# Attention scores by half blocks of queries in array quarters, one double bank per step

## The chip, the cores and the metric

The kernel runs on one core of a Trainium2 chip. The metric is device time in microseconds, the median over runs. Engines are named as in the profile: PE (matmul), PEld (its weight loads), DVE (vector), ACT (scalar), POOL (GpSimd), SP (the queue that issues most transfers).

## What is computed

Windowed attention with four sink keys, then a mixture of experts over its output, all in float32:

```python
B, H, S, D = 4, 8, 768, 64          # n_sink = 4, window = 128
scores = q @ k^T / sqrt(D)
keep = (key < n_sink) | ((0 <= query - key) & (query - key < window))
a = softmax(where(keep, scores, -1e9))
x = (a @ v) as (B * S, H * D) = (3072, 512)
logits = x @ w_gate + log1p(exp(x @ w_noise)) * noise   # 8 experts, top 2, softmax of the two
out = sum over the two experts: weight * (relu(x @ w1[e]) @ w2[e])    # 512 -> 1024 -> 512
```

## The kernel before, in words

Attention runs over 16 pairs of heads (g), each in three steps (jj): 48 steps (n). A step handles 256 queries (two blocks of 128, a = 0 and 1) of the two heads of its pair (h), which makes four units of 128 queries. A query block needs the keys of its own block and of the one before, and the four sinks.

In a step, `qk` (L389) makes the scores of one block a for both heads: the 64 rows of head h of the array hold 128 queries as weights, and 264 columns stream through (132 of the block before with the sinks, 132 of its own). The first block of a head pair has only its own 132. Each block's scores lie in one double bank of PSUM (`S`, one bank per head). `prev` (L392, ACT) copies the 132 old columns to the buffer `cbuf`; `cur` (L399, DVE) puts the own keys over the old ones where the mask `le` allows it (L397 for the first block of a pair). The 128 key slots of a unit are so used twice: an old key leaves the window exactly where an own key enters. `nosink` (L402) and `cur1` (L406), both on POOL, mend the sinks for the first blocks. Then follow `mins` (L409, DVE: row maxima, `mn`), `minus_max` (L412, POOL: `nb`), `exps_sums` (L423, ACT: four exponentials with their sums), `ptr` (L465, PE: eight transposes into bank `P`; L468 for the sinks' probabilities, copied by `pcopy`, L458, POOL), `ptr_c` (L474, ACT: `CT`), `ptr_m` (L484, POOL: `CM`, CT masked to the own keys), `pv` (L494 with v of the old block and L497 with `dv`, the difference of v between neighbouring blocks, made by `dv`, L300), `sinks` (L509), `pv_c` (L517, ACT: output to `xtn`) and `rows` (L523, DVE). After the last pair of a batch come the gate projection (L708), the routing and the writing of rows to memory; between the last steps the first expert rows are gathered. Then the expert stage begins (L1157 to L1229), in which PE multiplies to the end.

The order in attention is written out by hand: `Plan.op` records every operation with its engine, and `Plan.replay` issues them in the order of the table `ORDER`. Each engine works its instructions off in that order. Three double banks (`D`) serve scores, transposes and gate projections in turn, and `replay` picks the bank that is free first. `kind` tells which form of the array a PE operation uses; it enters only the durations with which the order is made. Loads of kq and v go through SP in the order of the table; a buffer of v (two of them) is loaded anew when the step that read it last is done.

## Time and profile before

| | |
|---|---|
| median of 3 runs | 753.51 us (750.51 to 756.1) |
| profiled execution | 756.2 us |
| its span, mean granted clock | 754.6 us, 0.988 |
| busy of the span: PE, PEld, DVE, ACT, POOL | 729.2, 618.4, 418.1, 339.5, 393.6 us |

The span runs from the first instruction to the last; the device time of the same execution is 1.6 us longer. A busy share is an average over two very different stages (attention to about 178 us, experts from there), so it is read by stretch. Matmuls overlap in the records, hence a busy PE may still have room. In the chain of waits a piece is named by its engine, tile and line, with the time it spends on the chain, which for instructions that overlap is their pace.

### The profile page before, as it was taken

Reading aid. Unit: us, or ns where it says so; the run is one execution under the profiler, and the core shown is the slowest. Engines: PE = TensorE matmul, PEld = TensorE weight load, DVE = VectorE, ACT = ScalarE, POOL = GpSimd, SP = SyncE. Lnnn points to the kernel's source line nnn. Section 1 sums busy time; section 2 is a strip of 40 time slices with the busy share of each in tenths; the row PEclk is TensorE's granted clock in tenths of the full one; section 3 lists DMA queues with packets and bytes.
Section 4 is the critical chain, followed back from the end, with each engine's and each line's share of the span. In section 5 each row is a group of like instructions: output and inputs, shape, how many; then the busy total and the mean of one; then the engine's idle time right before and its main releaser. Section 6 shows DMA issues by size and latency. Waiting matters only on the chain.

```text
span 754.6 us, 13413 instructions
## 1 busy us (share of the span) xinstructions
PE 729.2 (97%) x4787; PEld 618.4 (82%) x4787; DVE 418.1 (55%) x1082; ACT 339.5 (45%) x907; POOL 393.6 (52%) x640
## 2 busy tenths in 40 slices
PE   8999899889999999999999999999999999999995
PEld 4766666567889898889889988998899999999994
DVE  5779688786754654654365446535652664473420
ACT  5999799785224413341333243323432441343221
POOL 4346458771237385456636573747284755647212
PEclk9999899989999999999999999999999999999998
DMA  6557687945546743553445354526351653454033
GB/s 227 194 174 221 147 260 170 266 89 153 155 145 145 241 100 60 152 144 63 87 141 132 51 98 144 123 50 154 128 101 28 157 165 62 83 172 74 15 43 43
DMA packets 58310, 97.30 MB, mean 129 GB/s; under 512 B 19296, under 2 KB 31840, under 8 KB 58240
## 3 DMA queue, kind: packets, MB, share of 16 engines
q1 hardware_dynamic: 44864, 68.82, 30.3%
q0 software_dynamic: 13376, 27.60, 20.5%
q8 instruction: 38, 0.62, 0.4%
q14 instruction: 32, 0.26, 0.1%
HBM read 67.99 MB, written 28.40 MB: 128 GB/s over the span
## 4 chain that ended last, share of the span: by engine, by line
PE 77%; ACT 8%; issue 4%; DMA 4%; DVE 3%; POOL 2%; POOLq 0%; ACTq 0%; SPq 0%; DVEq 0%
PE H L1159 11%; PE H L1157 11%; PE H L1158 11%; PE Y L1224 11%; PE Y L1225 11%; PE Y L1223 11%; ACT cbuf L423 4%; PE D L389 3%; PE X L494 1%; ACT cbuf L392 1%; ACT CT L474 1%; PE Y L1228 1%; PE Y L1229 1%; POOL out L1247 1%; PE X L350 1%
## 5 line engine op out<-in xcount | busy, mean ns | idle before, releaser
L1008 POOL DMA_INDIRECT xg<-x_rows,rt_idq x174 | 174.2, 1001 | 60.9 <-issue 51.3
L1204 ACT ACTIVATE h<-H 128x384 fp32r<-128x384 f32 (+4 forms) x127 | 63.8, 503 | 254.5 <-PE H L1159 254.3
L1158 PE MATMUL H<-sqn,w 128*128 128x384 f32 (+4 forms) x508 | 174.0, 343 | 0.9 <-DVE sqn L300 0.9
L1157 PE MATMUL H<-skn,w 128*128 128x384 f32 (+4 forms) x508 | 174.5, 344 | 0.0
L1159 PE MATMUL H<-skn,w 128*128 128x384 f32 (+4 forms) x508 | 174.3, 343 | 0.0
L1212 DVE SCALAR_TENSOR_TENSOR h<-H,h 128x384 fp32r<-128x384 f32 (+4 forms) x167 | 75.1, 470 | 163.7 <-ACT h L1204 163.2
L1247 POOL DMA_INDIRECT out<-y,idx x53 | 93.7, 1767 | 50.5 <-ACT y L1232 34.9
L1256 POOL COPY spacer<-h 1x1 f32<-1x1 f32 x88 | 28.0, 319 | 147.4 <-ACT h L1204 147.2
L1158 PEld LDWEIGHTS H<-sqn,w 128*128 128x128 f32 x508 | 95.4, 188 | 7.7 <-DVE sqn L300 1.2
L1157 PEld LDWEIGHTS H<-skn,w 128*128 128x128 f32 x508 | 95.4, 188 | 7.4 <-ACT skn L1075 0.4
L1159 PEld LDWEIGHTS H<-skn,w 128*128 128x128 f32 x508 | 95.3, 188 | 2.1
L423 ACT ACTIVATE cbuf<-cbuf,nb 128x132 f32<-128x132 f32 x192 | 75.6, 412 | 2.4 <-POOL nb L412 2.4
L1225 PE MATMUL Y<-w2a,h 128*128 128x512 f32 x192 | 75.6, 394 | 0.0
L1225 PE MATMUL Y<-w2b,h 128*128 128x512 f32 x192 | 75.6, 394 | 0.0
L1224 PE MATMUL Y<-w2a,h 128*128 128x512 f32 x192 | 75.5, 393 | 0.0
L1224 PE MATMUL Y<-w2b,h 128*128 128x512 f32 x192 | 75.5, 393 | 0.0
L1223 PE MATMUL Y<-w2b,h 128*128 128x512 f32 x192 | 75.1, 391 | 0.0
L1223 PE MATMUL Y<-w2a,h 128*128 128x512 f32 x192 | 74.8, 389 | 0.0
L389 PE MATMUL D<-kq 64*128 64x264 f32 (+1 forms) x384 | 57.1, 406 | 9.2 <-DVE cbuf L399 3.6
L1075 ACT ACTIVATE skn<-xtn 128x512 fp32r<-128x512 f32 (+2 forms) x46 | 27.8, 605 | 58.5 <-DVE xtn L1066 58.4
L389 PEld LDWEIGHTS D<-kq 64*128 64x128 f32 x384 | 31.6, 192 | 21.1 <-DVE cbuf L399 6.0
L399 DVE COPY_PREDICATED cbuf<-le,D 128x256 f32<-128x256 uint8 x80 | 34.7, 445 | 18.4 <-ACT cbuf L392 17.8
(210 smaller groups left out, 1203.8 us busy)
## 6 DMA issues: line engine op xcount, KB each, us to landing
st<-in_w1l SPq DMA_DIRECT2D x32, 512.0 KB, 4.4
st<-in_w2l SPq DMA_DIRECT2D x32, 512.0 KB, 4.1
kq<-in_kq SPq DMA_DIRECT2D x15, 792.0 KB, 6.5
out<-zt SPq DMA_DIRECT2D x31, 256.0 KB, 5.6
vn<-in_v SPq DMA_DIRECT2D x16, 384.0 KB, 5.8
x_rows<-xr SPq DMA_DIRECT2D x48, 128.0 KB, 5.0
xg<-x_rows,rt_idq POOLq DMA_INDIRECT x174, 2.8
out<-y,idx POOLq DMA_INDIRECT x53, 5.1
```

Of the source, the lines that this page charges most:

```text
L389: nc.tensor.matmul(p[:, :2 if j else 1], kq(g)[r, j // 2, 2 + j % 2, NS:], x[:, :2 if j else 1], start=True, stop=True)
L423: nc.scalar.activation(C(n)[:, u], C(n)[:, u], AF.Exp, bias=get("nb", n)[:, u:u + 1], scale=1.0 / math.sqrt(D), accum_out=get("sm", n // 2 ...
L1008: nc.gpsimd.indirect_dma_start(out=x[:, i, :], out_offset=None, in_=xbuf.rearrange("r (q d) -> (r q) d", d=sh.SW), in_offset=bass.Indirect ...
L1157: nc.tensor.matmul(p, w[:, 0], xh, start=(i == 0), stop=False)
L1158: nc.tensor.matmul(p, w[:, 0], xl, start=False, stop=False)
L1159: nc.tensor.matmul(p, w[:, 1], xh, start=False, stop=(i == sh.DM // 128 - 1))
L1204: nc.scalar.activation(get("h", FC * q + f, [128, 2 * 128 * FIRST], F32R)[:, :width], H(q, f), AF.Relu)
L1212: nc.vector.scalar_tensor_tensor(h[:, o:o + s1 - s0], p[:, s0:s1], 0.0, h[:, s0:s1].bitcast(F32), op0=OP.max, op1=OP.subtract)
L1223: nc.tensor.matmul(p, hh, w[:, 0], start=(f == 0), stop=False)
L1224: nc.tensor.matmul(p, hh, w[:, 1], start=False, stop=False)
L1225: nc.tensor.matmul(p, hl, w[:, 0], start=False, stop=(f == FC - 1))
L1247: d = nc.gpsimd.indirect_dma_start(out=out, out_offset=bass.IndirectOffsetOnAxis(ap=c["idx"][:size(e, t), e, t:t + 1], axis=0), in_=get("y ...
```

## The change

The 128 queries of a block are split in halves (i). A score matmul now uses a quarter of the array: 64 rows of head h by 64 columns of queries, and 196 key columns. For the first half these are the old block, the sinks and the own block's first 64 keys in one piece; for the second half the last 64 old keys with the sinks (68 columns) and then all 128 own keys, whose first 64 are written straight over slots that the window has left. Scores of a whole step lie in one double bank, one bank per head. `prev` becomes one copy of four units (132 columns each), `cur` two predicated copies, each of 64 partitions, all units and 64 columns. The first block of a pair gets one addition of a mask (`cur0`), and `nosink` goes. kq is laid out anew in memory for this, with as many bytes.

The order is new throughout. `SIDE` says for some operations which of two engines they go to, and `BANKS` which bank each use takes. `dv` is on POOL for all pairs (before, for every second two), `ptr_m` on DVE for four of every twelve steps. By `SIDE`, 5 of 48 score copies, 2 CT copies and 5 output copies move from ACT to DVE, 9 `pcopy` from POOL to ACT, and 12 `minus_max`, 6 additions to the sums and one `cur1` from POOL to DVE. In front of the diff's core the tables themselves are left out.

```diff
-PR = dict(load_qk=0.0, load_v=24.264, w1=36, pc_pool=0, gap_8=1, dv_pool=2, et=42, cm_pool=12, gap=4, subs=0)
+PR = dict(load_qk=0.0, load_v=24.264, w1=36, pc_pool=0, gap_8=1, dv_pool=4, et=42, cm_pool=8, gap=4, subs=0)
...
 ORDER = """
...
+"""
+SIDE = """
...
+"""
+BANKS = """
...
 """
...
+        if alt:
+            self.alts.append((i, (eng, dur, kind), alt))
+            if SIDE.replace("\n", "")[len(self.alts) - 1:len(self.alts)] == "1":
+                eng, dur, kind = alt
+            fn.__defaults__ = fn.__defaults__[:-1] + (eng,)
...
-                    x = self.slot[kx] = len(r) - 1 if kx in last else min(range(len(r)), key=lambda x: r[x])
+                    x = self.slot[kx] = int(banks[len(self.slot)]) if banks else len(r) - 1 if kx in last else min(
+                        range(len(r)), key=lambda x: r[x])
...
-                d = (d + (0 if k % 3 == kind % 3 else .2 if k == 1 else .15)) * (2 if t < self.cold else 1)
+                d = (d + (0 if k % 4 == kind % 4 else .2 if k == 1 else .15)) * (2 if t < self.cold else 1)
...
-    def qk(n, a):
-        g, j, _ = at(n, 2 * a)
-        for h in range(2):
-            r = slice(h * D, (h + 1) * D)
-            p = get("S", 2 * n + a, [128, 2, 512], F32, "ps")[:, h, :2 * KW].rearrange("p (a b) -> p a b", a=2)
-            x = keys(g, max(j - 1, 0))[r]
-            nc.tensor.matmul(p[:, :2 if j else 1], kq(g)[r, j // 2, 2 + j % 2, NS:], x[:, :2 if j else 1], start=True, stop=True)
-
-    def prev(n, a):
-        nc.scalar.activation(C(n)[:, 2 * a:2 * a + 2, :], get("S", 2 * n + a)[:, :, :KW], AF.Copy)
-
-    def cur(n, a):
-        c, p = C(n)[:, 2 * a:2 * a + 2, NS:], get("S", 2 * n + a)
-        if at(n, 2 * a)[1] == 0:
-            nc.vector.tensor_tensor(c, p[:, :, NS:KW], m0[:, None, :].to_broadcast([128, 2, 128]), op=OP.add)
+    def scores(n):
+        return get("S", n, [128, 2, 512], F32, "ps")[:, :, :2 * BW].rearrange("p h (a k) -> p a h k", a=2)
+
+    def qk(n):
+        for a in range(2):
+            g, j, _ = at(n, 2 * a)
+            for i in range(2):
+                for h in range(2):
+                    r, t = slice(h * D, (h + 1) * D), slice(64 * i, 64 * i + 64)
+                    k, x = kq(g)[r, 0].rearrange("p b k -> p (b k)"), scores(n)[t, a, h]
+                    w, k0 = kq(g)[r, 1, j, t], KW * (j - 1)
+                    if not j or not i:
+                        o = x if j else x[:, :KW]
+                        nc.tensor.matmul(o, w, k[:, k0:k0 + BW] if j else k[:, :KW], start=True, stop=True)
+                    else:
+                        nc.tensor.matmul(x[:, 64:KW], w, k[:, k0 + 64:k0 + KW], start=True, stop=True)
+                        y = x[:, :64]
+                        y = bass.AP(tensor=y.tensor, offset=y.offset, ap=[list(y.ap[0]), [KW, 2], [1, 64]])
+                        nc.tensor.matmul(y, w, k[:, k0 + KW:k0 + KW + 128].rearrange("p (a k) -> p a k", a=2), start=True, stop=True)
+
+    def moved(eng, out, x):
+        if eng == "DVE":
+            nc.vector.tensor_copy(out, x)
         else:
-            nc.vector.copy_predicated(c, le[:, None, :].to_broadcast([128, 2, 128]), p[:, :, KW + NS:2 * KW])
-
-    def nosink(n):
-        nc.gpsimd.memset(C(n)[:, :2, :NS], -BIG)
-
-    def cur1(n):
-        c = C(n)[:, 2:, NS:2 * NS]
-        nc.gpsimd.tensor_tensor(c, c, m1[:, None, :].to_broadcast([128, 2, NS]), op=OP.add)
+            nc.scalar.activation(out, x, AF.Copy)
+
+    def small(eng):
+        return nc.gpsimd if eng == "Pool" else nc.vector
+
+    def old(n):
+        return int(n % NJ == 0)
+
+    def units(n):
+        return C(n).rearrange("p (a h) k -> p a h k", a=2)
+
+    def prev(n, eng):
+        moved(eng, units(n)[:, old(n):], scores(n)[:, old(n):, :, :KW])
+
+    def cur0(n):
+        nc.vector.tensor_tensor(units(n)[:, 0], scores(n)[:, 0, :, :KW], m0[:, None, :].to_broadcast([128, 2, KW]), op=OP.add)
+
+    def cur(n, i):
+        r = slice(64 * i, 64 * i + 64)
+        c = units(n)[r, old(n):, :, r]
+        nc.vector.copy_predicated(c, le[r, None, None, :].to_broadcast([64, 2 - old(n), 2, 64]), scores(n)[r, old(n):, :, KW:])
+
+    def cur1(n, eng):
+        c = C(n)[:, 2:, :NS]
+        small(eng).tensor_tensor(c, c, m1[:, None, :].to_broadcast([128, 2, NS]), op=OP.add)
...
+            need = {jj, max(jj - 1, 0)}
+            op("PE", .68 if jj else .61, n + P(g, "qk"), lambda n=n: qk(n), r=[("kq", g, i) for i in need], w=[("S", n)],
+               u=[("kq", g), ("C", n)], kind=3)
+            op("ACT", .46 if jj else .27, n + P(g, "prev"), lambda n=n, e=0: prev(n, e), r=[("S", n)], w=[("C", n, 0)], u=[("C", n)],
+               alt=("DVE", .61 if jj else .34, 0))
             if not jj:
-                op("Pool", .05, n + P(g, "nosink"), lambda n=n: nosink(n), w=[("C", n, 0)], u=[("C", n)])
-            for a in range(2):
-                z = n + .2 * a
-                s = 2 * n + a
-                need = [jj] if not jj or a else [jj - 1, jj]
-                op("PE", .45 if jj or a else .26, z + P(g, "qk"), lambda n=n, a=a: qk(n, a),
-                   r=[("kq", g, i) for i in {jj, *need}], w=[("S", s)], u=[("kq", g), ("C", n)], kind=1)
-                if jj or a:
-                    op("ACT", .27, z + P(g, "prev"), lambda n=n, a=a: prev(n, a), r=[("S", s)], w=[("C", n, a)], u=[("C", n)])
-                op("DVE", .335, z + P(g, "cur"), lambda n=n, a=a: cur(n, a), r=[("S", s)], w=[("C", n, a)], u=[("C", n)])
+                op("DVE", .34, n + P(g, "cur"), lambda n=n: cur0(n), r=[("S", n)], w=[("C", n, 0)], u=[("C", n)])
+            for i in range(2):
+                op("DVE", .335 if jj else .2, n + P(g, "cur"), lambda n=n, i=i: cur(n, i), r=[("S", n)], w=[("C", n, 0)], u=[("C", n)])
             if not jj:
-                op("Pool", .15, n + .4 + P(g, "cur1"), lambda n=n: cur1(n), w=[("C", n, 1)], u=[("C", n)])
-            op("DVE", .62, n + .4 + P(g, "mins"), lambda n=n: mins(n), r=[("C", n, 0), ("C", n, 1)], w=[("mn", n)], u=[("C", n)])
+                op("Pool", .15, n + .4 + P(g, "cur1"), lambda n=n, e=0: cur1(n, e), w=[("C", n, 0)], u=[("C", n)], alt=("DVE", .085, 1))
...
+               alt=None if odd else ("DVE", .6, 0))
...
+    kq = np.zeros((B * HP, 128, 2, NB, 128 + NS), np.float32)
+    for i, x in enumerate((k, q)):
+        kq[:, :, i, :, :128] = x.reshape(B, HP, 2, NB, 128, D).transpose(0, 1, 2, 5, 3, 4).reshape(B * HP, 128, NB, 128)
+    kq[:, :, 0, :, 128:] = kq[:, :, 0, :1, :NS]
```

How the rows stand on the engines. SP at the start of the program (vr are the sinks' values), before:

```order
L356 DMA vr<-in_vs 16x1024 x2
L367 DMA vn<-in_v 128x768
L364 DMA kq<-in_kq 128x528 x3
L364 DMA kq<-in_kq 128x1584 x2
L367 DMA vn<-in_v 128x768
L690 DMA nz<-in_noise 128x192
```

and now:

```order
L379 DMA kq<-in_kq 128x2x264 x3
L379 DMA kq<-in_kq 128x1584
L382 DMA vn<-in_v 128x768
L379 DMA kq<-in_kq 128x1584
L371 DMA vr<-in_vs 16x1024 x2
L382 DMA vn<-in_v 128x768
L728 DMA nz<-in_noise 128x192
```

The loads of kq, which stood behind vr and the first v, are the queue's first.

PE in attention, some four steps after the first gate projection, before (L389 scores, L465 and L468 transposes, L494 and L497 the products with v, L509 sinks):

```order
L465 MATMUL D<-idf,cbuf 128x64 x8
L389 MATMUL D<-kq 128x264 x4
L465 MATMUL D<-idf,cbuf 128x64 x8
L468 MATMUL D<-idf,pcbuf 128x64 x2
L389 MATMUL D<-kq 128x264 x4
L465 MATMUL D<-idf,cbuf 128x64 x8
L494 MATMUL X<-CT,vn 64x128 x4
L497 MATMUL X<-CM,dv 64x128 x4
```

and now, at about the same step (L406 to L411 scores, L500 and L503 transposes, L529 and L532 products with v, L544 sinks):

```order
L544 MATMUL X<-ps,vr 128x128 x4
L500 MATMUL D<-idf,cbuf 128x64 x16
L503 MATMUL D<-idf,pcbuf 128x64 x2
L406 MATMUL D<-kq 64x196 x2
L408 MATMUL D<-kq 64x68
L411 MATMUL D<-kq 64x2x64
L408 MATMUL D<-kq 64x68
L411 MATMUL D<-kq 64x2x64
L406 MATMUL D<-kq 64x196 x2
L408 MATMUL D<-kq 64x68
L411 MATMUL D<-kq 64x2x64
L408 MATMUL D<-kq 64x68
```

What was four matmuls per step among the transposes is now a run of twelve, in pieces of 196, 68 and 2x64 columns, in an array form of its own.

ACT at about the same steps, before (L392 score copies, L423 exponentials, L474 CT, L501 sinks' probabilities, L517 output):

```order
L474 ACTIVATE CT<-D 128x512
L392 ACTIVATE cbuf<-D 128x2x132
L423 ACTIVATE cbuf,sm<-cbuf,nb 128x132 x4
L501 ACTIVATE ps<-D 128x128
L474 ACTIVATE CT<-D 128x512
L392 ACTIVATE cbuf<-D 128x2x132 x2
L517 ACTIVATE xtn<-X 128x256 x2
L423 ACTIVATE cbuf,sm<-cbuf,nb 128x132 x4
L392 ACTIVATE cbuf<-D 128x2x132
```

and now (L417 stands for every plain copy, L458 exponentials, L536 sinks' probabilities):

```order
L417 ACTIVATE cbuf<-D 128x4x132
L458 ACTIVATE cbuf,sm<-cbuf,nb 128x132 x4
L417 ACTIVATE xtn<-X 128x256 x2
L417 ACTIVATE CT<-D 128x512
L417 ACTIVATE cbuf<-D 128x4x132
L417 ACTIVATE cbuf<-D 128x2x132
L458 ACTIVATE cbuf,sm<-cbuf,nb 128x132 x4
L417 ACTIVATE CT<-D 128x512
L536 ACTIVATE ps<-D 128x128
```

Two copies of 2x132 elements have become one of 4x132; the rest of a step's work on ACT stands there as before.

## Rows read from the trace of the kernel before

**Rows 1.** Busy time of each engine by stretch (us, count), granted clock, DMA share

```profile
core 0: us, PE busy (x) PEld busy (x) DVE busy (x) ACT busy (x) POOL busy (x), PEclk, DMA share, GB/s
...
20.00:40.00 20.00, 19.77 (x256) 14.68 (x254) 14.54 (x37) 19.95 (x86) 7.34 (x27) 1.00 0.55 186
...
60.00:80.00 20.00, 18.76 (x259) 14.05 (x259) 18.61 (x69) 19.64 (x85) 12.82 (x37) 1.00 0.75 175
...
140.00:160.00 20.00, 15.83 (x172) 11.05 (x172) 16.21 (x67) 17.25 (x67) 15.40 (x40) 0.91 0.44 120
...
sum 180.00, PE 163.41 PEld 115.03 DVE 132.45 ACT 152.34 POOL 99.49; mean PE 18.16 PEld 12.78 DVE 14.72 ACT 16.93 POOL 11.05
...
176.00:746.00 570.00, 568.80 (x2859) 505.47 (x2858) 288.75 (x687) 188.09 (x298) 293.15 (x378) 1.00 0.46 110
```

**Rows 2.** Chain of waits, 14 to 76 us (start us, us, what)

```profile
19.43 0.48 ACT CT L474
...
21.91 0.55 ACT cbuf L392 x2
22.45 1.50 ACT cbuf L423 x8
...
25.03 0.27 ACT xtn L517
```

**Rows 3.** Chain of waits, 46 to 60 us

```profile
47.96 1.16 PE D L389 x8
...
49.36 0.59 PE X L494 x8
49.95 0.44 PE X L497 x8
...
52.99 0.87 PE D L389 x8
53.86 0.24 PE D L465 x8
```

**Rows 4.** PE in order of time, 50.31 to 50.34 us

```profile
50.31 0.42 PE L708 MATMUL D<-xtn,wbd 128*32 128x256 f32 x4
```

**Rows 5.** Groups, 0 to 180 us (count, busy us, mean ns, idle before)

```profile
L789 ACT ACTIVATE rt_ex<-rt_ab 128x48 f32<-128x48 f32 x3 | 0.7, 244 | 0.4 <-DVE rt_ab L787 0.3
...
L399 DVE COPY_PREDICATED cbuf<-le,D 128x256 f32<-128x256 uint8 x80 | 34.7, 445 | 18.4 <-ACT cbuf L392 17.8
...
L397 DVE TENSOR_TENSOR cbuf<-D,m 128x256 f32<-128x256 f32 x16 | 6.7, 419 | 4.7 <-PE D L389 3.8 <-ACT cbuf L423 0.5
L300 DVE TENSOR_TENSOR dv<-vn 128x640 f32<-128x640 f32 x8 | 6.5, 812 | 2.8 <-DMA vn<-in_v 2.8
...
L300 DVE TENSOR_TENSOR sqn<-D,skn 128x512 fp32r<-128x512 f32 x4 | 2.7, 676 | 0.3 <-ACT skn L1075 0.3
...
L450 DVE RECIPROCAL ri<-sm 128x4 f32<-128x4 f32 x16 | 1.8, 153 | 0.5 <-POOL sm L436 0.5
...
L484 POOL TENSOR_SCALAR_AFFINE_SELECT CM<-CT 128x512 f32<-128x512 f32 x32 | 21.3, 666 | 9.5 <-ACT CT L474 3.7 <-issue 3.0 <-POOL CM L484 0.8
L300 POOL TENSOR_TENSOR dv<-vn 128x640 f32<-128x640 f32 x8 | 12.4, 1546 | 4.2 <-DMA vn<-in_v 4.2
```

**Rows 6.** POOL's waits, 14 to 178 us (total, times, longest), and landing of v

```profile
POOL dv L300 <- DMA vn<-in_v: 2.1, 2, 1.3
...
DMA to landing us min/median/max: 3.4/5.8/9.6
```

**Rows 7.** SP in order of time, and the chain of waits, start

```profile
0.93 0.87 SPq L356 DMA_DIRECT2D vr<-in_vs  x2
...
2.30 2.33 SPq L364 DMA_DIRECT2D kq<-in_kq  x5
...
1.25 5.42 PE X L350 x13
```

**Rows 8.** Chain of waits, 70 to 86 us

```profile
75.60 6.11 DMA vn<-in_v
```

## What the change is predicted to do

> **What bounds the kernel now.** I first read the busy time of each engine by stretch [rows 1]. From 176 us to 746 us PE is busy 568.80 of 570 us at granted clock 1.00: that is the expert stage, and the change does not touch it. The change lives in the attention stage, roughly the first 178 us, so it can only move the moment at which the expert matmuls begin; whatever it gains there comes off the end one for one, and nothing else does. Within attention the reader is to see two halves. From 20 to 80 us ACT has no idle time: 19.95 us of the first 20, 19.64 of the last. PE is close behind (19.77 and 18.76, though matmuls overlap in these figures), and DVE goes from 14.54 to 18.61. After that no engine is full all the time: at 140 to 160 us ACT shows 17.25, DVE 16.21, PE 15.83 of 20, with a granted clock of 0.91. Then I read the chain of waits. In the first half it runs along ACT nearly without a break: four exponentials with their sums take 1.50, two score copies 0.55, a copy of turned probabilities 0.48, a copy of the output 0.27 [rows 2]. In the second half it jumps between engines and includes pure transfer waits such as 6.11 us for v at 75.60 [rows 8]. So the first half is a matter of ACT work, the second of PE work, of order and of late transfers. All sums are made against the profiled execution, 756.2 us (span 754.6); the median of the runs shown, 753.51, lies 2.7 below it.
>
> **The change part by part.** *Score matmuls.* A full step now streams 2 blocks of 264 columns, two head halves side by side; eight instructions take 0.87 us when PE is in the right array form already, 1.16 when it enters it after a wait [rows 3]. That is 0.22 us per 264-column pass. With 196 columns a pass is 0.22 x 196/264 = 0.163, and a quarter streams four of them in a step: 0.65. Two of the quarters have each pass in two pieces (68 and 128 columns). Small passes cost little beside their columns: eight transposes of 64 columns, two side by side, take 0.24 [rows 3], so 0.060 a pass where 64 columns stream in 0.053; four more pieces add 4 x 0.007, which makes 0.68. [...] This holds if the four quarters run side by side. For that the trace has a near relative: the gate projection puts four column strips of the array to work, and all four first passes fall in one window of 0.03 us [rows 4]. So a full step saves 0.87 - 0.68 = 0.19, times 32 = 6.1 us; the 16 first steps of a head pair (132 and 264 columns before, 132 and 196 now) save 2 x 0.22 x 68/264 = 0.11 each, 1.8 in all. Together -7.9 us of PE.
>
> *Array forms.* Before, scores, transposes and sinks use one form of the array (64 rows by 128 columns, or 16 of them), so PE goes from one to another without a break: the transposes behind the scores take 0.24 for eight [rows 3]. Now scores have a form of their own. Counted along PE's order, changes of form in attention go from 128 to 149. The price of one is read from two neighbours of the same size: the eight matmuls of CT, entered from the transposes, take 0.59, the eight of CM behind them 0.44 [rows 3], so 0.15. 21 x 0.15 = +3.2 us. Net on PE: -7.9 + 3.2 = -4.7. Bounds: -1.8, if a change is as dear as the 1.16 row makes it (21 x 0.29 = 6.1), and -7.9, if it is entered for nothing. In the first half PE hides behind ACT; half of the steps, -2.3, fall in the second, where PE shares the chain. I take -1.5.
>
> *ACT.* One copy of 528 elements replaces two of 264. Two of them take 0.55 [rows 2], a copy of 512 takes 0.48, so one of 528 about 0.50: -0.05 a step. Of 80 short copies 13 short and 30 long remain: 22.0 becomes 18.6. Two CT copies (0.48) and five output copies (0.27) go to DVE: -2.3. Nine small copies of sink probabilities come from POOL; the nearest ACT row is a 128x48 exponential, 0.244 [rows 5]: +2.2. ACT loses 3.5 us in all. Counted along the table SIDE, 2.9 of these lie in the first 24 steps, where ACT sets the pace: 0.8 from merging, 2.8 from moved copies, less 0.7 for three sink copies. On the path I take -2.5, between -1.0 (the merging alone) and -3.5.
>
> *DVE.* It gets sixteen masks of turned probabilities (12 of 512 elements at 0.676, as the subtraction that reads PSUM, and 4 of 256 at 0.419), +9.8; it loses eight v differences (0.812), -6.5; ten PSUM copies come in, +6.1 by the same two rows; nineteen tiny operations at 0.153, +2.9 [rows 5]. The predicated copies stay at 256 elements per partition, since a half block uses 64 partitions and all four units: 64 of them at 0.445 and 32 of half the size (between 0.25 and 0.445, I take 0.31) for 80 before, +2.8. Together +15 on the 132.45 of the first 180 us [rows 1]. ACT hides this where DVE stands at 14.54 of 20, but not at 60 to 80 us. There four steps' masks (2.4) come in and two v differences (1.6) go out: +0.8. That is what I take; bounds 0, and +5 if a third of it lands on the path.
>
> *POOL.* All sixteen v differences are now its own, +8 x 1.546 = 12.4, against sixteen masks of at most 0.666 and some forty operations of about 0.2 that leave. Its sum falls a little. But each difference waits for a v transfer, whose median is 5.8 us from issue to landing [rows 6], and behind it on POOL stand the negated maxima, for which ACT's exponentials wait. Before, behind the start, POOL waited 2.1 us for v in two places [rows 6] and DVE 2.8 [rows 5], and DVE's waits stop the score buffers: the 6.11 us in [rows 8] ends in such a difference, with predicated copies queued behind it. I take 0: the same lateness moves from one queue to another. Bounds: -4.9 (both sums gone) and +10 (the POOL rival below, less the part that ACT's queue absorbs).
>
> *Start.* kq is now issued ahead of the sink values and v; its issues began at 2.30 us, and the queue's first at 0.93 [rows 7]: up to -1.4. The warming matmuls ahead of the first scores fall from 13 to 5; 13 of them take 5.42 us, to 6.67 [rows 7], with the first scores right behind them, so scores no longer wait for them. But five end at 3.3 us, and the first scores may then run at the lower clock level: up to +2.0 for three steps of 0.68. I take -0.8. The buffers change too (one double bank per step instead of two), which removes waits of scores for a bank; these are short in the first half and I price them at nothing, since ACT is full there.
>
> Sum: -1.5 (PE) -2.5 (ACT) +0.8 (DVE) +0 (POOL) -0.8 (start) = **-4.0 us**. 756.2 becomes 752.2; on the median 753.5 becomes 749.5.
>
> **The rivals.** *More than that.* Part of the second half are waits of an engine's whole queue for a transfer, as the 6.11 us for v [rows 8]. The order is new everywhere, so such a wait could vanish (-5 of it, since v is needed some time anyway), and PE's full -4.7 count instead of -1.5: 753.5 - 4.0 - 5 - 3.2 = 741.3. For it: DVE no longer holds v differences at all. Against it: other waits may appear, and v loads stand no further ahead of their use than before.
>
> *Nothing to be had.* Scores get cheaper, but ACT, not PE, evacuates them at 19.9 of 20; only merging helps, -0.8 to -1.0, and DVE's +0.8 eats it: 753.5. [...] The full ACT in [rows 1] agrees for the first half.
>
> *Slower through POOL.* Fourteen v differences behind the first two each wait for their transfer on POOL, and negated maxima, exponentials, transposes follow late. It decides from 0.8 us per group on: 14 x 0.8 = 11 us outweighs the 4.0 by more than 7.5. At 1.0 us per group: 753.5 - 4 + 14 = 763.5. For it: 2.1 us over two waits is 1.05 each [rows 6]. Against it: only two of the eight differences on POOL waited behind the start.
>
> *Slower through the passes.* If a quarter's two passes go before the next quarter starts, the overlap is mostly lost: eight quarter blocks of 0.163 are 1.3 us instead of 0.68, 0.43 above the 0.87 of before; 48 x 0.43 + 3.2 = 24 us, of which PE's slack hides some: 753.5 + 18 = 771. With part of the overlap lost PE loses from 0.80 us a step on (3.2/48 = 0.07 below 0.87); midway, at 1.0, it is 48 x 0.13 + 3.2 = 9.4, about 762. [...] Four first passes inside 0.03 us [rows 4] speak against it, though there the strips are columns alone, not quarters.
>
> **How the numbers follow.** The three runs before span 750.51 to 756.1, so about 1% (7.5 us) is what can be told from no change. Forecast (-8 to 0): 0.54. More than that: 0.25. Nothing to be had: 0.09. POOL: 0.07. The passes: 0.05. Faster by over 1% (below 746.0) is the second case and the lowest edge of the first: 0.28. Slower (above 761.0) is the two last, nearly whole: 0.11. Within: 0.61. The range reaches down to the second case, 741, and up to where POOL's waits just eat the gain and DVE's +5 is added, 758; it leaves out some 0.1 on either side. The forecast's own range is 745 to 753.
>
> **What would show it.** In the profile after: score matmuls of a full step in some 0.7 us behind one another (1.1 or 1.3 shows the passes' case); long score copies of about 0.50 pace on ACT; ACT still 19 or more of 20 from 20 to 70 us, with the expert matmuls beginning near 174 instead of 178; DVE near 147 us in its first 180; POOL's waits for v near 5 us in all (14 shows the POOL case). Wrong would be the forecast if ACT has room from 20 to 80 us: then something else sets the pace, and my ACT and PE terms change places.

## The result and the profile after

The changed kernel takes 758.5 us (median of 20 runs, 755.07 to 765.51) against 753.5 for the one before (20 runs beside them): a ratio of 1.0069, 95% interval 1.0050 to 1.0087. A second set gave 760.07 against 755.52, ratio 1.0064 (1.0035 to 1.0093). So it is slower by 0.7%, about 5 us, where 4 us less had been forecast. That is inside the 1% called no change, and just above the range (758.0). One yardstick for all that follows: the kernel before, measured against itself on the same chip, gave 0.9966 (0.9943 to 0.9989), an interval that leaves out 1 though both kernels are the same. So ratios that differ by less than some 0.35% (2.6 us) are not told apart here.

The profiled execution is the shortest of the twenty: 755.07 us, span 753.5. It is even 1.1 us shorter than the profiled one of before. Its rows show how the work changed; how much time the change costs they do not show, and this is a first lesson of the case. These are the stretches that answer to [rows 1] (columns: length, busy time and count of each engine, granted clock, DMA share, GB/s):

```profile
core 0: us, PE busy (x) PEld busy (x) DVE busy (x) ACT busy (x) POOL busy (x), PEclk, DMA share, GB/s
...
20.00:40.00 20.00, 19.55 (x356) 15.87 (x351) 18.04 (x46) 17.27 (x71) 7.55 (x16) 1.00 0.52 162
40.00:60.00 20.00, 16.64 (x312) 12.34 (x310) 16.90 (x42) 18.46 (x78) 8.39 (x21) 1.00 0.78 226
60.00:80.00 20.00, 18.38 (x363) 14.75 (x359) 18.55 (x68) 19.34 (x78) 11.22 (x27) 1.00 0.85 199
...
100.00:120.00 20.00, 14.51 (x274) 11.98 (x275) 16.90 (x64) 16.28 (x64) 14.60 (x34) 0.91 0.59 157
...
sum 180.00, PE 154.15 PEld 116.55 DVE 152.34 ACT 148.05 POOL 90.08; mean PE 17.13 PEld 12.95 DVE 16.93 ACT 16.45 POOL 10.01
...
176.00:746.00 570.00, 566.74 (x2831) 504.56 (x2831) 287.01 (x683) 186.90 (x296) 294.51 (x377) 1.00 0.47 110
```

The reader is to see that the work moved the way that the forecast gave: PE from 163.41 to 154.15, ACT from 152.34 to 148.05, DVE from 132.45 to 152.34. But ACT, 19.95 of 20 before, has room at 20 to 60 us, and no engine took its place: PE, DVE and ACT all stand between 16.6 and 19.6. The prediction had named just this as the sign that it was wrong.

The chain of waits, which ran along ACT in [rows 2], now winds through DVE with its masks and predicated copies:

```profile
31.78 0.61 ACT cbuf L417
...
32.43 0.61 ACT CT L417
...
33.06 0.69 DVE CM L516
...
33.78 0.47 DVE cbuf L437
...
34.28 0.70 DVE mn L444
...
35.01 0.44 DVE xtn L415
...
35.47 0.77 DVE xr L558 x2
```

The scores themselves did what they were priced at. Here are two full steps in a row, PE in order of time (start, length, line, operation, count):

```profile
66.78 0.46 PE L500 MATMUL D<-idf,cbuf 64*128 64x64 f32 x8
67.17 0.38 PE L406 MATMUL D<-kq 64*64 64x196 f32 x2
67.19 0.34 PE L408 MATMUL D<-kq 64*64 64x68 f32 x4
...
68.42 0.38 PE L411 MATMUL D<-kq 64*64 64x128 f32 x3
68.73 0.46 PE L500 MATMUL D<-idf,cbuf 64*128 64x64 f32 x8
```

From 67.17 to 68.73 are 1.56 us for two steps. A single step followed at once by other matmuls takes 0.88 to 0.89 from its first start to the next one's, so the second step costs 0.67 to 0.68 (forecast: 0.68) and the change of array form 0.21. Of the 32 full steps 17 stand alone in PE's order; such a step takes no less than the 0.87 of [rows 3]. The matmuls of the two columns of quarters start 0.02 us apart (67.17 and 67.19).

And the groups of the first 180 us that answer to [rows 5] (shapes, count, busy, mean ns, idle before):

```profile
L437 DVE COPY_PREDICATED cbuf<-le,D 64x256 f32<-64x256 uint8 x64 | 28.5, 454 | 2.3 <-ACT cbuf L417 1.2
L437 DVE COPY_PREDICATED cbuf<-le,D 64x128 f32<-64x128 uint8 x32 | 9.6, 301 | 0.4
...
L516 DVE TENSOR_TENSOR CM<-D,ge 128x512 f32<-128x512 f32 x12 | 8.3, 691 | 3.3 <-ACT CT L417 2.0 <-issue 0.7 <-PE D L500 0.4
...
L417 ACT ACTIVATE cbuf<-D 128x528 f32<-128x528 f32 x30 | 18.2, 611 | 7.5 <-PE D L411 7.1
...
L312 POOL TENSOR_TENSOR dv<-vn 128x640 f32<-128x640 f32 x16 | 24.8, 1550 | 4.5 <-DMA vn<-in_v 4.1 <-PE D L503 0.2
```

Each price in them is within 0.02 us of the one used; only the long copy's record lasts 0.61 us, but where work follows at once, the next instruction mostly starts 0.49 to 0.52 us after it (forecast: 0.50). POOL waits 4.1 us for v, some 5 were forecast.

### The profile page after: what moved, and what is told of

Same layout as the page of the kernel before. It is cut to its first block, busy times and chain, and to the rows that moved or that the text cites. A ratio compares the mean times of both kernels' runs of the same rounds, so it can differ in the third digit from the quotient of the medians.

```text
span 753.5 us, 14768 instructions
## 1 busy us (share of the span) xinstructions
PE 717.7 (95%) x5491; PEld 618.5 (82%) x5491; DVE 437.4 (58%) x1139; ACT 334.8 (44%) x872; POOL 386.1 (51%) x588
## 4 chain that ended last, share of the span: by engine, by line
PE 74%; DVE 10%; ACT 7%; issue 5%; DMA 2%; POOL 1%; POOLq 0%; DVEq 0%; ACTq 0%
PE H L1195 11%; PE H L1197 11%; PE H L1196 11%; PE Y L1262 11%; PE Y L1263 11%; PE Y L1261 10%; ACT cbuf L458 3%; DVE cbuf L437 2%; DVE mn L444 2%; DMA st<-in_w1l 2%; PE D L406 1%; DVE xr L558 1%; PE Y L1266 1%; POOL out L1285 1%; PE Y L1267 1%
## 5 line engine op out<-in xcount | busy, mean ns | idle before, releaser
L1046 POOL DMA_INDIRECT xg<-x_rows,rt_idq x174 | 176.0, 1011 | 61.1 <-issue 51.4
L458 ACT ACTIVATE cbuf<-cbuf,nb 128x132 f32<-128x132 f32 x192 | 75.3, 403 | 5.9 <-POOL nb L447 4.0
L406 PE MATMUL D<-kq 64*64 64x196 f32 (+1 forms) x448 | 41.5, 339 | 3.9 <-DVE cbuf L437 1.2
L312 DVE TENSOR_TENSOR w<-st,w 128x1024 fp32r<-128x1024 f32 x30 | 36.7, 1223 | 13.9 <-ACT w L1151 13.4
L1183 DVE TENSOR_TENSOR gw<-xg,perm 32x8 f32<-32x8 f32 x174 | 27.5, 158 | 26.0 <-DMA xg<-x_rows,rt_idq 21.9
```

The lines of the kernel that those rows point to most:

```text
L406: nc.tensor.matmul(o, w, k[:, k0:k0 + BW] if j else k[:, :KW], start=True, stop=True)
L458: nc.scalar.activation(C(n)[:, u], C(n)[:, u], AF.Exp, bias=get("nb", n)[:, u:u + 1], scale=1.0 / math.sqrt(D), accum_out=get("sm", n // 2 ...
L1046: nc.gpsimd.indirect_dma_start(out=x[:, i, :], out_offset=None, in_=xbuf.rearrange("r (q d) -> (r q) d", d=sh.SW), in_offset=bass.Indirect ...
```

## The experiments

All medians are device microseconds beside runs of the kernel before on the same chip. The first two rows repeat the result.

| kernel | median | before | ratio (95%) |
|---|---|---|---|
| changed | 758.5 | 753.5 | 1.0069 (1.0050 to 1.0087) |
| after_again | 760.07 | 755.52 | 1.0064 (1.0035 to 1.0093) |
| before_again | 752.82 | 755.89 | 0.9966 (0.9943 to 0.9989) |
| form_only | 755.61 | 755.89 | 0.9990 (0.9969 to 1.0012) |
| order_only | 764.86 | 755.89 | 1.0112 (1.0086 to 1.0137) |
| keep_busy | 762.86 | 755.89 | 1.0081 (1.0056 to 1.0107) |
| dv_dve | 761.66 | 755.35 | 1.0085 (1.0052 to 1.0119) |
| side0 | 762.33 | 755.35 | 1.0091 (1.0062 to 1.0119) |
| cm_pool | 760.37 | 755.35 | 1.0073 (1.0045 to 1.0102) |
| moves_only | 766.16 | 755.35 | 1.0150 (1.0109 to 1.0191) |
| mid_order | 758.68 | 755.52 | 1.0039 (1.0018 to 1.0061) |
| tail_order | 759.89 | 755.52 | 1.0054 (1.0034 to 1.0074) |
| mid_tail | 757.92 | 755.52 | 1.0032 (1.0006 to 1.0058) |
| act_twice | 764.77 | 752.80 | 1.0160 (1.0142 to 1.0177) |
| dve_twice | 769.08 | 752.80 | 1.0203 (1.0173 to 1.0233) |
| pe_twice | 769.03 | 752.80 | 1.0206 (1.0181 to 1.0232) |
| before_act_twice | 767.98 | 752.80 | 1.0179 (1.0133 to 1.0226) |
| form_nb | 761.73 | 754.00 | 1.0113 (1.0086 to 1.0139) |
| before_nb | 753.45 | 754.00 | 1.0003 (0.9979 to 1.0027) |

**The three parts apart.** The change has a form (quarters, one bank, merged copies), an order, and moves of work between engines. In form_only the changed kernel's operations stand at the places that before's order gives them, on the engines of before:

```diff
-PR = dict(..., dv_pool=4, ..., cm_pool=8, ...)
+PR = dict(..., dv_pool=2, ..., cm_pool=12, ...)
 ORDER: each operation at the place of its counterpart in the order of before
 SIDE:  all 0;  BANKS: whichever is free
```

> The new form of the scores alone (quarters, 196 columns, one bank per step, merged copies), in the order of before and with every operation on the engine that had it before. If the form is what it was priced at: PE -4.7 of which 1.5 on the path, ACT -0.8 by merging, DVE's smaller predicated copies up to +2.8 busy, so 751 to 754 us, ratio 0.996 to 1.001. If the form is what costs (changes of array form, passes in turn, predicated copies on half the partitions): ratio 1.007 or more, like the whole change.

Measured 755.61, ratio 0.9990 (0.9969 to 1.0012): the form alone changes nothing that can be told, though the 2.3 us that the forecast had for it (1.5 for PE, 0.8 for merging) lie just at the edge of the interval. order_only has the new order and form with the engines of before (the same lines of PR and SIDE, ORDER as changed except that eight masks stand behind the copy they then read, BANKS as changed).

> The new form and the new order, with every operation on the engine that had it before (half of the v differences back on VectorE, all masks on GpSimd, the 40 moved operations moved back). If the moves onto VectorE cost (its busy time in the first 180 us went from 132 to 152 us): 2 to 5 us below the changed kernel, ratio 0.999 to 1.004. If the moves paid, as I had forecast for ScalarE (-2.5): 2 to 4 us above the changed kernel, ratio 1.010 to 1.012.

It is 0.45% above the changed kernel, little more than the yardstick: 1.0112 against 1.0069 and 1.0064. So the moves seem to pay some 3.4 us within the new order, and the new order with the old engines costs 9 us over form_only. moves_only is form_only with the moves (dv_pool=4, cm_pool=8, SIDE as changed, masks on DVE right behind their copies).

> The new form and the engines of the change (all v differences on GpSimd, a third of the masks on VectorE, the 40 moved operations), but in the order of before; banks taken as they come free. It is form_only plus the moves. If the new order by itself is what costs, and the moves pay as they did between order_only and the changed kernel (some 4 us): 750 to 753 us, ratio 0.993 to 0.998, faster than both. If moves and order only work together: 756 us or more, ratio 1.002 or more.

With the moves in the old order the kernel loses 10.5 us against form_only (766.16 to 755.61), where 750 to 753 us had been expected of the moves alone. Either alone is dear, 9 and 10.5 us, and together they cost 5. The order was made for the moved work, and neither can be priced by itself. What is shown is that order and moves together cost the 0.7%, and that the form does not. The table of banks belongs to the order and was not tried by itself.

**The moves one by one.** dv_dve changes `dv_pool=4` to 2 alone, cm_pool changes `cm_pool=8` to 12 and puts eight masks behind the copy they then read, side0 puts the 40 ones of SIDE to 0.

> The changed kernel with half of the v differences back on VectorE, as before; nothing else. In the trace of the changed kernel one of them holds GpSimd for 1.51 us at 103.43, and behind it a negated maximum comes late, ScalarE waits 1.7 us for that, TensorE stands for 2.9 us and its clock falls. Theory A (such differences on GpSimd cost where a maximum waits behind them): 1 to 3 us below the changed kernel, ratio 1.003 to 1.006. Theory B (VectorE is the bound, and eight differences of 0.81 are 6.5 us more for it): 2 to 5 us above it, ratio 1.009 to 1.013.

> The changed kernel with the 40 operations of the table of sides back on the engines that had them before (copies on ScalarE, sums, negations and sink copies on GpSimd); the v differences and the masks stay where the change put them. If these moves off ScalarE pay (forecast: 2.8 us of its first 24 steps): 2 to 4 us above the changed kernel, ratio 1.010 to 1.012. If VectorE is the bound of the first half now (18.0 of 20 us at 20 to 40): 1 to 4 us below, ratio 1.002 to 1.005.

> The changed kernel with all masks of turned probabilities on GpSimd, as before; they read the copy that ScalarE makes, not the bank. Takes 10 us from VectorE and gives GpSimd sixteen operations of 0.41 to 0.65. If VectorE is the bound: 1 to 4 us below the changed kernel, ratio 1.002 to 1.005. If GpSimd's queue is what delays (negated maxima behind long operations there): 1 to 5 us above, ratio 1.008 to 1.013.

1.0085, 1.0091, 1.0073: all at or above the changed kernel, none of them clear of it. Taking back no single one of the moves helps. That does not show that they cost nothing where they are, since work taken back burdens another queue: in cm_pool ACT waits 7.9 us for negated maxima from POOL, in the changed kernel 4.0 (first 180 us).

**The clock.** Each run lists the mean granted clock. In the twenty runs of the changed kernel the span grows by 0.72 us for each us of clock lost (span times one minus the clock), correlation 0.91 (0.84 us in the runs of before, correlation 0.80). This is read from the spread of the runs; no run sets the clock by itself. before_again is the kernel before, unchanged; keep_busy adds dummies to the changed one:

```diff
     def ptr(n):
         p = get("P", n, [128, 2, 512], F32, "ps")
+        for i in range(2 if n >= 24 else 0):
+            nc.tensor.matmul(p[:, 1], cst["one"], cst["one"][:, None, :].to_broadcast([128, 4, 128]), start=True, stop=True)
```

> The kernel before, unchanged, to get the granted clock of many of its runs. In twenty runs of the changed kernel the span goes with the clock: from 754.4 us at 0.996 to 763.9 at 0.98, some 0.7 us of span for each us of clock that is lost (1 minus the clock, times the span). Theory A (the change loses work time and also lets the clock fall more often): the runs of before show a median clock near 0.992 to 0.994, and at an equal clock they lie some 2 us below the changed kernel. Theory B (the clock is the same and all 5 us are work): median clock 0.988 as in the changed kernel, and at equal clock 5 us below it.

> The changed kernel with two more dummy matmuls of 512 columns ahead of the transposes of each of the last 24 steps; they write the bank that the transposes then overwrite, so they run in TensorE's waits, and cost at most 24 x 0.43 = 10 us where it does not wait. If falls of the granted clock after TensorE's pauses cost the time (0.72 x 9 us lost in the median run): median clock 0.992 or more, 2 to 6 us below the changed kernel, ratio 0.999 to 1.004. If the clock is not the cause: no gain, ratio 1.007 to 1.02.

The changed kernel lost a mean of 8.9 us of clock in 20 runs and 11.1 in 12 more; before lost 7.6 over the 119 runs of it that list their clock. The difference of 2.1 is worth 0.72 x 2.1 = 1.5 us. With 0.72 times the lost clock taken off each span, the changed kernel stands at 750.9 and 750.6, before at 747.8: some 3.0 us are work (2.7 with 0.84 in place of 0.72). Theory A, then, with both parts. By the same subtraction form_only stands at 749.1, order_only at 754.4 and moves_only at 753.7 (6.8, 11.4 and 14.5 us of clock lost): only about half of what order and moves cost alone is work. The dummies did raise the clock (6.3 us lost), but the time did not fall (0.1 to 0.2% above, which can't be told from no change), as was expected if the clock is not the cause. With the clock taken off, keep_busy stands at 756.6: some 6 of the 10 us of dummy work came through, more than 0.72 x 3.4 = 2.4 us could return. So this run neither shows nor refutes the share of the clock.

**Two places in the new order.** By a count of finished attention work the profiled execution is some 3 us ahead of before at 105 us (maxima, exponentials, copies, masks, differences and routing steps; 1 us without the routing), and by 110 us nothing of this is left. In another order such a count is a rough measure. PE there, and POOL and DVE just before:

```profile
105.59 0.45 PE L866 MATMUL D<-m,one 128*128 128x56 bf16 x12
108.98 0.46 PE L500 MATMUL D<-idf,cbuf 64*128 64x64 f32 x8 [2.95 <-DVE rt_ro L923]
110.26 0.59 PE L406 MATMUL D<-kq 64*64 64x196 f32 x2 [0.82 <-DVE cbuf L437]
```

```profile
102.79 0.64 POOL L519 TENSOR_SCALAR_AFFINE_SELECT CM<-CT 128x512 f32<-128x512 f32 x1 [0.79 <-ACT CT L417]
103.39 1.54 POOL L312 TENSOR_TENSOR dv<-vn 128x640 f32<-128x640 f32 x1
104.91 0.22 POOL L447 TENSOR_SCALAR nb<-mn 128x4 f32<-128x4 f32 x1
```

```profile
102.33 0.69 DVE L444 TENSOR_REDUCE mn<-cbuf 128x4 f32<-128x528 f32 x1
...
103.80 1.20 DVE L851 TENSOR_TENSOR m<-oh 128x48 bf16<-128x48 f32 x1
```

The maxima are done at 103.0, their negation waits until 104.91 behind a mask and a v difference of 1.54, and the exponentials, an output copy, the row transposes and a bank's release on DVE follow late in turn, each first in its own queue. PE stands for 2.95 us. The eight transposes right behind that still take 0.46, as elsewhere; behind one more wait of 0.82 the granted clock is 0.50, and a 196-column score matmul takes 0.54 to 0.59 instead of 0.33 to 0.38 (columns as in the stretches above, the clock is the 0.50):

```profile
111.00:112.00 1.00, 1.00 (x26) 1.00 (x23) 0.91 (x4) 0.15 (x2) 0.90 (x5) 0.50 0.06 16
```

after_again shows whether that belongs to the order:

> The changed kernel, unchanged, for a second profiled execution and for more granted clocks beside runs of before on the same chip. The first profiled execution was the shortest of twenty (755.07 us, clock 0.994) and was 6 us ahead of before at 105 us, then gave it back between 105 and 118 us and after the last exponential. If those two places belong to the order: the same two places lose again (TensorE idle for 2 us or more between 100 and 116 us, 11 us or more from the last exponential to the first expert matmul, 7.2 in the order of before), and the median is 757 to 760 us. If they were chance: other places, and a median nearer to that of before.

It does; the median, 760.07, is just above what was expected. PE in the second execution (span 758.6):

```profile
110.04 0.46 PE L500 MATMUL D<-idf,cbuf 64*128 64x64 f32 x8 [2.94 <-DVE rt_ro L923]
...
179.47 0.69 PE L1195 MATMUL D<-skn,w 128*128 128x512 f32 x1
...
183.19 0.40 PE L1195 MATMUL D<-skn,w 128*128 128x512 f32 x1
...
190.16 0.18 PE L860 MATMUL X<-m,tri 128*128 128x48 bf16 x1 [1.32 <-DVE m L851]
```

The pause recurs to 0.01 us. Here the first expert matmuls, too, ran longer (0.62 to 0.69 us instead of 0.40, with a granted clock of 0.70 from 180 to 185 us), and the routing of the last block comes so late that PE waits 1.32 us in the middle of the expert stage (1.36 in the first execution), which it never does there before. The forecast had left that stage out. The v difference on POOL is not the whole of the pause: in dv_dve, where this one is back on DVE, PE stands there for 2.00 us.

```profile
113.02 0.69 PE L500 MATMUL D<-idf,cbuf 64*128 64x64 f32 x8 [2.00 <-DVE rt_ro L923]
```

mid_order moves six operations near 105 us:

```diff
 POOL  ... CM(29)  dv(10)  nb(30) ...      ->  CM(29)  nb(30)  dv(10)
 ACT   ... w<-st   CT(29) ...              ->  CT(29)  w<-st
 DVE   xr(28) xr(29) mn(31) vm rt_ro ...   ->  mn(31) vm rt_ro xr(28) xr(29)
```

> The changed kernel with six operations moved in its order, all around 101 to 108 us: the negated maxima of step 30 stand ahead of the v difference on GpSimd, the expert weight conversion behind the copy of step 29 on ScalarE, and on VectorE the maxima of step 31 and the two routing operations that free a bank stand ahead of two row transposes. If the local order is what makes TensorE stand there and its clock fall: TensorE's pause of 2.9 us goes, 2 to 4 us below the changed kernel, ratio 1.001 to 1.005. If the time is only put off to the tail: within 1 us of the changed kernel.

tail_order puts the last 189 operations in the relative order of before, with a bank table that fits them, and mid_tail does both.

> The changed kernel with its last 189 operations (from about step 44 on) in the relative order of before; engines, form and all before that as changed. If the order of the tail costs (11.5 us from the last exponential to the first expert matmul, 7.2 in the order of before): that stretch falls to 7 to 9 us, the time by 2 to 4 us against the changed kernel, ratio 1.001 to 1.005. If the tail is long because the engines were given other work (masks on VectorE): it stays at 11 us or more and the time does not fall.

> Both moves of order in one kernel (the six operations near 105 us, and the last 189 in the order of before). If both places cost by themselves and add up: 4 to 7 us below the changed kernel, 752 to 755 us, ratio 0.997 to 1.000. If one hides behind the other: no better than the better of the two.

In mid_order the pause shrinks and the clock holds in this stretch (PE in order of time, then the stretch from 100 to 120 us):

```profile
107.92 0.47 PE L500 MATMUL D<-idf,cbuf 64*128 64x64 f32 x8 [0.59 <-DVE rt_ro L923]
109.85 0.38 PE L406 MATMUL D<-kq 64*64 64x196 f32 x2 [1.47 <-DVE cbuf L437]
```

```profile
100.00:120.00 20.00, 14.88 (x305) 11.69 (x299) 18.04 (x68) 17.32 (x71) 14.39 (x35) 1.00 0.65 185
```

The ratio falls to 1.0039, a point 0.3% below the changed kernel, at the edge of what can be told. But the execution shown does not begin its experts earlier for it: the first expert matmul starts at 180.62, at 177.03 and 179.47 in the two executions of the changed kernel, and from 160 to 180 us the granted clock is 0.74.

```profile
180.62 0.48 PE L1195 MATMUL D<-skn,w 128*128 128x512 f32 x1
```

The tail is a misreading of mine. From the last exponential to the first expert matmul the changed kernel needs 11.5 us (ACT, then PE):

```profile
165.36 0.19 ACT L458 ACTIVATION_READ_ACCUMULATOR cbuf<-cbuf,nb 128x1 f32 x1
```

```profile
177.03 0.48 PE L1195 MATMUL D<-skn,w 128*128 128x512 f32 x1
```

In tail_order it is 7.7, but the last exponential itself comes 8 to 10 us later than in the two executions of the changed kernel. In that order it stands near the end of the stage (at 171.5 and 172.5 us in before, too), so this stretch tells where an order puts it and not what the tail costs:

```profile
175.70 0.18 ACT L458 ACTIVATION_READ_ACCUMULATOR cbuf<-cbuf,nb 128x1 f32 x1
```

```profile
183.55 0.50 PE L1195 MATMUL D<-skn,w 128*128 128x512 f32 x1
```

1.0054: nothing that can be told. Both together, 1.0032, are 0.35% below the changed kernel, and with the clock taken off 748.5 against 750.6 and 750.9 (mid_order 750.2, tail_order 749.6). The local order of these places may therefore hold about 2 of the 3 us of work, which is indicated and not shown, and neither place can be given a share of it.

**Who sets the pace.** Three kernels put known work on one engine in steps 3 to 23 of the changed kernel, one does so with ACT before. The work is done twice and writes the same values (two of the 21 second copies of act_twice fall on DVE, where SIDE has put the copy):

```diff
 act_twice, before_act_twice:   each copy of prev(n) twice, if 3 <= n < 24
 dve_twice:                     copy_predicated of cur(n, 1) twice, if 3 <= n < 24
 pe_twice:                      for a in (0, 1, 0, 1) if 3 <= n < 24 else range(2):     (in qk)
```

> The changed kernel with each copy of old scores on ScalarE made twice in steps 3 to 23 (the second writes the same values): some 8 us more of ScalarE in the first half. If ScalarE still sets the pace there (as the forecast had it): 6 to 8 us above the changed kernel, ratio 1.014 to 1.017. If it has room: less than 3 us above, ratio under 1.011.

> The changed kernel with the second predicated copy of each of the steps 3 to 23 made twice: 14 x 0.45 + 7 x 0.30 = 8.4 us more of VectorE in the first half. If VectorE sets the pace there now (its busy share is 18.0 of 20 us, and half of the v differences put back on it made step 24 come 4 us later): 6 to 8 us above the changed kernel, ratio 1.014 to 1.017. If not: less than 3 us, ratio under 1.011.

> The changed kernel with the score matmuls of steps 3 to 23 made twice: 21 x 0.65 = 13.7 us more of TensorE in the first half. The forecast let TensorE's savings count for a third in all and for nothing in the first half; then the time rises by less than 4 us, ratio under 1.012. If TensorE paces the first half: 10 to 14 us, ratio 1.019 or more.

> The kernel before with each copy of scores on ScalarE made twice in steps 3 to 23: 14 x 0.55 + 7 x 0.28 = 9.7 us more of ScalarE, which was busy 19.9 of 20 us there. If ScalarE set the pace of the first half before: 8 to 10 us above before, ratio 1.010 to 1.013. If even there a later wait takes it up: less than 4 us, ratio under 1.005.

Against a changed kernel at 1.0067, ACT's 8 us cost 7.0, DVE's 8.4 cost 10.3, PE's 13.7 cost 10.5. Each of these costs is uncertain by some 2 to 3 us. Before, ACT's 9.7 cost 13.5, part of it through the clock (11 to 12 with the clock taken off):

```profile
40.00:60.00 20.00, 18.03 (x176) 13.33 (x172) 10.08 (x25) 17.40 (x69) 7.04 (x22) 0.74 0.37 129
```

After the change work added to any of the three comes through at 0.8 to 1.2 us for one. That refutes each theory of one bound for the changed kernel, mine included. Before, ACT's added work comes through as well, as assumed; but no run put work on PE or DVE there, so that ACT alone set the pace is not shown. My reading, argued and not shown: a step's work passes through PE, ACT, DVE, POOL, ACT, PE in turn, each engine takes its queue in order, and what is added anywhere makes the step longer and pushes all behind it.

**Where the form's savings went.** In form_only ACT waits 8.6 us for negated maxima, where before it waited 2.4 and 3.1 in two executions. Its waits for scores went the other way, from 13.8 and 11.8 to 9.8, which is where PE's saving shows (ACT's waits, first 180 us: total, times, longest; before, then form_only):

```profile
ACT cbuf L392 <- PE D L389: 13.8, 11, 5.4
ACT cbuf L423 <- POOL nb L412: 2.4, 4, 1.4
```

```profile
ACT cbuf L414 <- PE D L408: 9.8, 9, 4.8
ACT cbuf L455 <- POOL nb L444: 8.6, 10, 1.6
```

One merged copy must see all scores of a step, and both predicated copies then wait for it; before, the first half's went on while the second half was copied (it began at 47.45 us, the second copy ended at 47.83). If that longer chain were the cause, a shorter link should pay. form_nb and before_nb put all negated maxima on DVE, right behind the maxima:

```diff
-        small(eng).tensor_scalar(get("nb", n, [128, 4]), get("mn", n), -1.0 / math.sqrt(D), ...)
+        nc.vector.tensor_scalar(get("nb", n, [128, 4]), get("mn", n), -1.0 / math.sqrt(D), ...)
```

> The new form in the order of before (form_only) with the negated maxima of all 48 steps on VectorE, right behind the maxima, instead of on GpSimd: some 48 x 0.08 us more of VectorE, and one change of engine less between a step's scores and its exponentials. In form_only ScalarE waits 8.6 us for these maxima, before 2.4. Theory A (the merged copy makes a step's chain longer, and the freed time of ScalarE turns into this wait): 2 to 5 us below form_only, ratio 0.993 to 0.997. Theory B (the wait only stands in for another): within 1 us of form_only, ratio 0.998 to 1.001.

> The kernel before with the same move of all 48 negated maxima to VectorE. Theory A: there ScalarE waits only 2.4 to 3.1 us for them, so at most 2 us below before, ratio 0.998 to 1.000, clearly less than what form_nb gains. If it gains as much as form_nb, the shorter chain is good in any form and says nothing on merging.

form_nb became slower by 9 us (1.0113 against 0.9990; on another chip, and with 12.0 us of clock lost instead of 6.8), before_nb did not change, and ACT waits as long as ever, now for DVE:

```profile
ACT cbuf L455 <- DVE nb L444: 10.0, 10, 2.1
```

Theory A in this form falls. Shown is that in form_only ACT waits less for scores and longer for maxima; that the savings went there is a reading, and why the maxima are late in that order stays open.

## Why the prediction was wrong, step by step

- **The sum as a whole.** It added five terms, each with a share "on the path", and had no term for the order. The order was in it only as a chance of gain ("a wait could vanish") and in the buffers ("price them at nothing"). This is the step that failed. What the runs showed in its place: the form gives nothing that can be told (-0.1%), order and moves together +0.8%, in sum +0.7%, about 5 us. Taken one after the other this is +1.2% and -0.45% (order first) or +1.6% and -0.8% (moves first), so the two do not add up as terms of a sum. Why the new order loses is indicated for a part (the places near 105 us and in the tail) and stays open for the rest.
- **PE, -1.5.** The price was right, 0.68 a step and 0.21 for a change of form (forecast: 0.15). PE is 9.3 us less busy where 4.7 net was expected (1.9 of it in the warming matmuls, 10.9 to 9.0). Of a share on the path nothing showed: with ACT's merging it would be -2.3 in form_only, and -0.8 came, with 1.6 either way, so a small share is not excluded. With the clock taken off form_only stands at 749.1, not below before (747.8).
- **ACT, -2.5.** Its cause, ACT at 19.95 of 20, fits before (before_act_twice). It did not carry over: once DVE and the order were changed too, ACT had room from the start. The moves of SIDE, for which 1.7 was taken, gave 1.8 inside the new order by side0, which can't be told from nothing; all moves together gave 3.4 there and cost 10.5 in the old order.
- **DVE, +0.8.** Its busy time rose by 19.9, not 15 (the "ten PSUM copies" are twelve, as the +6.1 has them; the tiny operations took 0.16 to 0.38, not 0.153). The table of waits shows a wait that I had not priced: where a mask on DVE and a copy on ACT read the same bank, the copy began behind the mask, 2.0 us in five waits of the turned copies and 2.7 in four of the sink copies. One mask ran from 44.73 to 45.42 and the turned copy began at 45.51, with ACT idle for 0.91 before it. Why the two did not run side by side the rows do not show. cm_pool, without these masks on DVE, is no faster, but there ACT waits longer for maxima.

```profile
ACT ps L536 <- DVE CM L516: 2.7, 4, 0.8
ACT CT L417 <- DVE CM L516: 2.0, 5, 0.9
```

- **POOL, 0.** Waits for v were right (4.1 us). What was missed near 105 us is the length of the difference itself: 1.54 us in a queue in which a maximum waits. dv_dve, without eight of them on POOL, is no faster, so this is one piece of the order and not a term of its own. The rival through POOL had that queue right and the reason, a late transfer, wrong; its threshold was a little off, too (14 x 0.8 - 4.0 is 7.2, not over 7.5).
- **Start, -0.8.** The first scores did run slower, 0.54 to 0.56 us for 196 columns in the matmuls that began up to 6.82 us and 0.33 to 0.35 from 7.20 on, though the granted clock reads 1.00 there. Even so the term is right or better as far as it can be seen: the first maxima stand at 7.0 us (6.7 to 7.2 in kernels with this start), 8.8 and 8.5 in the two executions of before. Whether this reaches the end was not tried.
- **Passes in turn** is refuted by 0.67 to 0.68 a step. Of the 1.1 and 1.3 us named as its sign the trace shows neither at a granted clock of 1.00, and no run shows where the 1.1 would come from.
- **Nothing to be had** (chance 0.09) is what the form alone gave, though not quite for its reason: in form_only ACT was busy 2.3 us less in the first 180 (150.00 against 152.34) and had room at 20 to 40 us (18.95 of 20).

## What to carry to other kernels

Where every engine works off a fixed order, a busy engine's price for added work need not be its price for removed work: ACT's 9.7 us added to before cost 13.5, and taking 8.4 us of PE and 2.3 of ACT out of it (form_only) gave less than can be told here. A new order is a term of the sum, with an error of its own size (5 us here with its moves, 9 with the old engines), even if its table only follows from the rest. And one profiled execution can stand at the end of its spread: compare mean clocks and a second trace before a difference of 0.5% is read out of two profiles.

## What the runs showed of the hardware

A VectorE operation of 48 elements took 1.20 us instead of 0.21 (the median of its four in the trace) while GpSimd's v difference of 1.54 us ran, and ended 0.07 us after it; in the second execution it took 1.21 us and ended 0.07 us after it again. A predicated copy beside the same v difference took 0.45, as elsewhere, so not every VectorE operation was held up. Work moved to GpSimd thus came with 0.99 us more in one operation of VectorE; why, the traces do not show. It was seen the other way, too: in dv_dve, beside a v difference on VectorE, the negated maxima took GpSimd 0.79 us instead of 0.23.

```profile
107.93 1.16 DVE L312 TENSOR_TENSOR dv<-vn 128x640 f32<-128x640 f32 x1
```

```profile
108.39 0.79 POOL L447 TENSOR_SCALAR nb<-mn 128x4 f32<-128x4 f32 x1
```

And where TensorE stood for 2.95 us in the changed kernel, the granted clock fell, though not at once: it was 1.00 from 109.0 to 109.5 us, just behind the pause, 0.62 in the next half microsecond, 0.50 from 110 to 113 and 0.98 from 113 to 114. The transposes behind the pause still took 0.46 us, the score matmuls after them 0.53 to 0.59 instead of 0.33 to 0.38, at the same place in both executions.
